# The order of attention's first loads, and where the second channel block's lag correlation is computed

## The chip, the cores and the metric

The kernel runs on one core of a Trainium2 chip. The metric is the device time of one launch in microseconds (us); the time given for a kernel is the median of its runs. The core has five engines that each work through their own list of instructions in order: TensorE (PE, matrix products), VectorE (DVE), ScalarE (ACT), GpSimd (POOL) and SyncE (SP, which does nothing but issue data transfers). A transfer (DMA) is issued by the queue of SP, ACT or POOL and then carried out by 16 DMA engines that all queues share. An instruction waits on semaphores for what it needs; what stands behind it in its list waits too.

## What is computed

The reference is a gated mix of two layers over the same input x (2048 positions, 576 channels), and the kernel returns the output and the gradient of every input for a given `grad_out`:

```python
def _A_ref(x, wqkv, wo):                       # attention, H = 32 heads of Dh = 18
    qkv = (x @ wqkv).reshape(B, S, 3, H, Dh).transpose(2, 0, 3, 1, 4)
    q, k, v = qkv[0], qkv[1], qkv[2]
    p = softmax(einsum("bhqd,bhkd->bhqk", q, k) * (Dh ** -0.5))
    o = einsum("bhqk,bhkd->bhqd", p, v)
    return o.transpose(0, 2, 1, 3).reshape(B, S, D) @ wo

def _B_ref(u, A_re, A_im, B_re, B_im, C_re, C_im, log_dt, Dskip):   # a state space layer, N = 128 states
    dt = exp(log_dt)[:, None]
    A = A_re + 1j * A_im;  Bc = B_re + 1j * B_im;  Cc = C_re + 1j * C_im
    P = exp((dt * A)[:, :, None] * arange(L))
    K = einsum("dn,dnl,dn->dl", Cc, P, dt * Bc).real     # one causal kernel of 2048 taps for each channel
    return causal_convolution(u, K) + u * Dskip

g = sigmoid((x * gate_w).sum(-1, keepdims=True))
out = g * _A_ref(x, ...) + (1 - g) * _B_ref(B_u, ...)
# returned: out, and the gradients of x, wqkv, wo, A_re ... Dskip and gate_w for grad_out
```

(The convolution is written with FFTs in the reference.)

## The kernel before

The kernel is one program of five stages. The order of instructions on each engine is written out by hand: in most of the kernel each engine runs what the source issues to it, in the order of the source.

**Stage s1** computes gate, queries, keys and values by matmuls on the transposed input, 24 steps in a row. The results are evicted by ACT and DVE to tiles `stg` and `qn` and stored in a DRAM tensor `QKV_d` (L409, L428) from the queues of ACT and POOL. Beside these steps run small jobs: the parameters of the state space layer (tiles `prm`, `zt`, `tp`, `Wn`, stored in `par_d` from POOL's queue), and `scale_go` (L293), which multiplies each 128-row tile of `grad_out` by g, for the gradient of attention, and by 1 - g. The second product, tile `xb`, is stored in DRAM in reversed order as `gyr_d` at L300: 16 stores of 144 KB from SP's queue. `gyr_d` is read later by the transfers that build `gyb_d` (in attention, from POOL's queue) and `RXn` (L592).

**Attention** goes through 32 units: 8 groups of 4 heads by 4 blocks of 512 queries. A unit has NST = 32 steps; NTOT = 1024 is the number of steps of all units. At each step G the forward pass computes one pair of score tiles (`ps_P<-QaT_g,KaT_g` on PE, Exp on ACT at L1382, then `accO` with the values `Vtok`). A second pass follows OFF = 39 steps later: transposed scores and Exp (L1387), the products with the output's gradient, `ds` on DVE (L1392), and the sums accV, accQ and accK. Part of each `ds` is transposed by a DMA on SP's queue (L1400, tile `dsT`), and accK waits for it. In the last unit the forward pass has ended: steps NTOT to NTOT + 62 hold only the second pass and the sums behind it. The operands of a group are loaded from `QKV_d` on SP's queue: `KaT` (keys with states on partitions, 4 tiles, `load_full`, L990 to L998), `QaT`, and `Vtok` (by a transposing DMA, `load_piece`). `at(("pre", G), f)` puts f at the head of step G; what has a time before step 0 is issued at once, in the order of its time. So the first loads on SP are KaT 0 to 3, Vtok 0, QaT 0, Vtok 1, Vtok 2.

**The S4 stage** treats the state space layer in 18 blocks of 32 channels. For each block b there is first its lag chain, which correlates x with the gated gradient at small lags, and which the rest of the block needs:

- `m_load(b)` loads `xs` (two transfers of 512 KB) and `gyp` (128 KB), L614 and L615;
- `m_part(b)` multiplies them on PE: 32 pairs of small matmuls into a PSUM tile `psM`; ACT copies it to `mst` (L628) and L629 stores that in DRAM (`Md_d`, 288 KB);
- `m_skw(b)` reads it back askew, in four transfers, as `skw` (L641);
- `m_sum(b)` sums it on PE with a 0/1 matrix, `misc<-sel,skw`;
- `m_fin(b)` puts the sums into two columns of `RX` on ACT (L652 to L654).

After that come `uv(b, 0)` and `uv(b, 1)` (PE `uvp<-RX,E1e`, ACT L708), which multiply the block's `RX` by the transposed basis `E1e` (made on PE by `turn_e` from `E1n`, which `load_en` or, for the first four halves, `en_first` loads in 4 pieces each); `scan_open(b)` copies the first column to `HG` (ACT, L714), and the scan on DVE (L733, L736, L738) runs over 15 segments. A block's second half of a scan runs together with the next block's first half. `xs`, `mst` and `skw` have one buffer each, `gyp` two.

Block 0's chain runs in attention's last unit: `m_load(0)` at NTOT + 15, `m_part(0)` at NTOT + 21 and `m_skw(0)` at NTOT + 25, and there the E1n pieces too (from NTOT + 23, one a step). `m_load(1)` comes at NTOT + 40, after the last of the `dsT` transposes. The rest of block 1's chain, and block 2's `m_load`, `m_part` and `m_skw`, are in the stage's prologue (L1452 to L1483), between the uv steps of blocks 0 and 1. From there on the loop over blocks keeps `m_part` and `m_skw` three blocks ahead of the scan and `m_load` four.

Of the kernel before, what the change touches and what calls it, by code (L numbers as in the profile page):

```python
# [20 lines left out]
def build(tc, aps, dbg_aps=None, stages=("s1", "attn", "post", "s4", "final")):  # L21
    nc = tc.nc
# [20 lines left out]
    NT = S // P  # L43
# [18 lines left out]
    with ExitStack() as gctx:  # L62
# [47 lines left out]
        gyr_d = dram.tile([P, NB, D], BF, name="gyr_d")  # L110
# [18 lines left out]
        with ExitStack() as ctx:  # L129
# [163 lines left out]
            def scale_go(b, q0):  # L293
                if q0 == 0:
                    dab[b] = s1.tile([P, TB, D], BF, tag="xr", bufs=4, name="d_a")
                for q in range(q0, q0 + 2):
                    t = b * TB + q
                    V.tensor_scalar(dab[b][:, q, :], xb[b][:, q, :], g_t[:, t:t + 1], None, op0=A.mult)
                    V.tensor_scalar(xb[b][:, q, :], xb[b][:, q, :], omg_t[:, t:t + 1], None, op0=A.mult)
                    nc.sync.dma_start(gyr_d[:, NT - 1 - t, :], xb[b][:, q, :])  # L300

            def da_turn(b, k, eng):
                if k < 2:
# [304 lines left out]
        def m_load(b, dma=nc.gpsimd.dma_start):  # L608
            xs = xss[b] = Q["pl"].tile([P, NSUB, SUB, CB], BF, tag="xs", bufs=1, name="xs")
            n = NSUB // 2  # L610
            for y in range(2):
                src = bass.AP(tensor=xb_d.tensor, offset=xb_d[b:b + 1, y * n:y * n + 1, 0:1].offset,
                              ap=[[XR * SUB * CB, NB], [SUB * CB, NSUB], [1, n * SUB * CB]])
                dma(xs[:, y * n:(y + 1) * n].rearrange("p e t c -> p (e t c)"), src)  # L614
            dma(Q["gyp2"][b % 2][:, SUB:2 * SUB, :].rearrange("p t c -> p (t c)"), gyb_d[b])  # L615
# [334 lines left out]
        if "attn" in stages:  # L950
# [5 lines left out]
            with ExitStack() as ctx:  # L956
# [33 lines left out]
                def load_full(g):  # L990
                    def piece(m):
                        t_ = grp_t.setdefault(g, {})["KaT", m] = ga.tile([P, KB], BF, tag="KaT", bufs=7, name="KaT_g")
                        nc.sync.dma_start(t_, strip("K", g, m * KB, KB))
                    for m in range(4):
                        if g == 0:
                            piece(m)
                        else:
                            at(("pre", 4 * NST * g + (16 if m == 3 else 6 * m - 59)), lambda m=m: piece(m))  # L998

# [121 lines left out]
                def at(n, f):  # L1121
                    todo.setdefault(n, []).append(f)
# [80 lines left out]
                def do_half(x):  # L1203
# [10 lines left out]
                    if odd:  # L1214
# [5 lines left out]
                        for y in range(2):  # L1220
                            nc.vector.tensor_copy(dOt[y][:, f0:f0 + fsz], dps[y][:, 0:fsz])
                            if u == 1:
                                nc.sync.dma_start(dO_d[:, t - 1 + y, :], dOt[y])

                load_full(0)
                lds = []
                for g in range(NG):
                    for m in range(4):
                        g0 = 4 * g * NST
                        lds += [(g0 + NST * m - 14, "QaT", g, m), (g0 + 8 * m - 18, "Vtok", g, m), (g0 + OFF + 8 * m - 18, "VaT", g, m),  # L1230
                                (g0 + OFF + 8 * m - 13, "Ktok", g, m), (g0 + OFF + NST * m - 14, "Qtok", g, m)]
                for g0, nm, g, m in sorted(lds):
                    if g0 < 0:
                        load_piece(nm, g, m)
                    else:
                        at(("pre", g0), lambda nm=nm, g=g, m=m: load_piece(nm, g, m))
# [33 lines left out]
                def en_first(b, h):  # L1270
                    enp[b, h] = load_en(b, h, nc.sync.dma_start, pieces=4)

                for x, f in ((15, lambda: pt_close("a", open_loads)), (15, lambda: m_load(0, nc.sync.dma_start)), (17, lambda: load_rx(0, nc.sync.dma_start)),
                             (21, lambda: m_part(0)), (23, lambda: pt_close("b", lambda: open_en(0))),
                             (25, lambda: m_skw(0)), (31, lambda: pt_close("c", lambda: open_en(1))),
                             (29, lambda: load_par(0, nc.sync.dma_start)), (33, lambda: load_par(1, nc.sync.dma_start)),
                             (OFF + NST // 16 - 1, lambda: m_load(1, nc.sync.dma_start))):
                    at(("pre", NTOT + x), f)
                for q, (b, h) in enumerate(((0, 0), (0, 1), (1, 0), (1, 1))):
                    at(("pre", NTOT + 23 + 4 * q), lambda b=b, h=h: en_first(b, h))  # L1280
                    for y in range(1, 4):
                        at(("pre", NTOT + 23 + 4 * q + y), lambda b=b, h=h, y=y: enp[b, h](y))
                for G in range(NTOT + OFF + 24):
                    now[0] = G
                    for f in todo.pop(("pre", G), []):
# [127 lines left out]
        if "s4" in stages:  # L1413
# [8 lines left out]
            with ExitStack() as ctx:  # L1422
# [27 lines left out]
                with tc.manual_schedule(engines={mybir.EngineType.SP}):  # L1450
# [6 lines left out]
                    turn_e(0, 0, 0, 4, dve_copy)  # L1457
                    m_sum(0)
                    m_fin(0)
                    uv(0, 0)  # L1460
                    prep_rx(1, dve_copy)
                    load_rx(1, nc.sync.dma_start)
                    turn_e(0, 1, 0, 4, dve_copy)
                    m_part(1)
                    m_skw(1)
                    m_load(2, nc.sync.dma_start)
                    uv(0, 1)
                    turn_e(1, 0, 0, 4, dve_copy)
                    scan_open(0)
# [1 line left out]
                    turn_e(1, 1, 0, 4)  # L1471
                    m_sum(1)
                    m_fin(1)
                    load_en(2, 1, nc.sync.dma_start)
                    uv(1, 0)
                    m_part(2)
                    m_skw(2)
                    uv(1, 1)
                    scan_open(1)
                    m_load(3, nc.sync.dma_start)  # L1480
                    prep_rx(2)
                    wk_cast(1)
                    for i in range(NBLK):  # L1483
# [387 lines left out]
```

## Time and profile before

| what | us |
|---|---|
| median of 3 runs | 2687.24 |
| lowest and highest run | 2683.43, 2697.16 |
| the profiled execution | 2685.73 |
| its span, first to last instruction | 2683.9 |
| PE busy in it | 2404.7 (90%) |
| ACT busy | 2350.8 (88%) |
| DVE busy | 2293.8 (85%) |
| POOL busy | 1818.0 (68%) |

The mean granted TensorE clock is 0.968 of the full one. On the time axis of the profiled execution, s1 ends near 120 us, attention runs from 131 to 2098, and the loop over blocks follows.

Some of the profile's views by stretch, as us of work in each window, with the clock granted to TensorE and the mean busy share of the DMA engines:

| window, us | PE | DVE | ACT | PE clock | DMA share |
|---|---|---|---|---|---|
| 118 to 120 | 0.67 | 1.36 | 1.10 | 1.00 | 0.37 |
| 121 to 131 | 0.09 | 0.00 | 0.52 | 0.50 | 0.94 |
| 131 to 141 | 9.97 | 1.65 | 5.92 | 0.50 | 0.03 |
| 141 to 160 | 18.32 | 5.85 | 15.35 | 1.00 | 0.35 |
| 2030 to 2096 | 44.84 | 40.25 | 31.12 | 0.66 | 1.10 |
| 2125 to 2131 | 4.79 | 1.55 | 2.88 | 0.51 | 1.03 |
| 2170 to 2192 | 20.89 | 21.40 | 20.27 | 1.00 | 0.83 |

A line of a timeline below has the start and the length of a group of instructions in us, the engine, the source line, the operation, the tiles written and read, and the count; in brackets stands how long the engine was idle before it and what ended the wait. The engines SPq, ACTq and POOLq in it are the queues that issue transfers. "L30" is the helper through which all matmuls go, so they are told apart by tile. A DMA share sums the times of packets, so it can go above 1.

### The profile page before, as it was taken

To read this page: it belongs to the slowest core of one execution; us is meant where nothing else is said; L and a number is where in the kernel's file an instruction comes from. 1 tells how busy PE (TensorE), PEld (TensorE's weight loads), DVE (VectorE), ACT (ScalarE), POOL (GpSimd) and SP (SyncE) were. 2 spreads that over 40 slices of the span, in tenths; PEclk is the share of its full clock that TensorE was granted. 3 is DMA by queue.
4 is the path that set the end of the run, shared out by engine and by line. 5 is a ranking of instruction groups with operands and counts; after the bars stand their busy time and mean duration, and the time that the engine had idled before them with its cause. 6 is when DMAs were issued, how large, how long until landed. Compare 5 with 4: busy or idle time off the path is not lost.

```text
span 2683.9 us, 69949 instructions
## 1 busy us (share of the span) xinstructions
PE 2404.7 (90%) x27411; PEld 1137.9 (42%) x27411; DVE 2293.8 (85%) x4090; ACT 2350.8 (88%) x2744; POOL 1818.0 (68%) x2829
## 2 busy tenths in 40 slices
PE   8799998998899899889888989989887699999999
PEld 4433333333333333333333333333232499998756
DVE  5648999999989999989999989989897589999964
ACT  5489999999999999999999999999995399999221
POOL 0278888888888888888888888887831045555431
PEclk9879999999999999999999999999996699999999
DMA  7637789879979978997898899789679889998895
GB/s 232 196 99 156 154 159 181 167 153 181 172 152 170 183 160 159 178 172 153 165 178 154 161 172 170 153 163 177 143 140 183 191 244 256 259 262 253 261 261 128
DMA packets 1157013, 486.63 MB, mean 181 GB/s; under 512 B 1071061, under 2 KB 1110598, under 8 KB 1154378
## 3 DMA queue, kind: packets, MB, share of 16 engines
q1 hardware_dynamic: 1110650, 341.49, 64.4%
q0 software_dynamic: 44016, 135.16, 18.3%
q10 hardware_dynamic: 2016, 5.51, 0.6%
q8 instruction: 214, 3.51, 0.6%
q14 instruction: 117, 0.96, 0.1%
HBM read 146.27 MB, written 93.80 MB: 89 GB/s over the span
## 4 chain that ended last, share of the span: by engine, by line
ACT 40%; PE 28%; DVE 18%; issue 6%; DMA 4%; POOL 2%; SPq 1%; ACTq 0%; DVEq 0%; POOLq 0%
ACT eb L1387 23%; ACT PT L1382 14%; DVE ds L1392 7%; PE ps_P L30 7%; PE accV L30 2%; PE ps_dx L30 2%; PE turn_p L1095 2%; PE ps_dwq L30 2%; DVE tz L733 2%; PE ps_proj L30 2%; DVE wab L753 2%; PE yp L30 2%; PE accK L30 1%; DVE dvacc L1149 1%; DVE tz L736 1%
## 5 line engine op out<-in xcount | busy, mean ns | idle before, releaser
L1392 DVE TENSOR_TENSOR ds<-ps_P,PT 128x512 bf16<-128x512 f32 x2048 | 1312.3, 683 | 125.5 <-PE ps_P L30 86.8
L1387 ACT ACTIVATE eb<-ps_P 128x1024 bf16<-128x1024 f32 x1024 | 1099.9, 1074 | 34.8 <-PE ps_P L30 34.5
L1382 ACT ACTIVATE PT<-ps_P 128x1024 bf16<-128x1024 f32 x1024 | 1105.0, 1080 | 21.7 <-PE ps_P L30 20.3
L30 PE MATMUL ps_P<-dOaT,VaT_g 32*128 32x512 bf16 x2048 | 581.9, 388 | 31.5 <-DVE ds L1392 16.1
L506 POOL TENSOR_TENSOR et<-eG,eT 128x448 f32<-128x448 f32 x576 | 542.2, 961 | 10.7
L30 PE MATMUL ps_P<-QaT_g,KaT_g 32*128 32x512 bf16 x2048 | 402.9, 386 | 136.5 <-ACT PT L1382 121.8
L30 PE MATMUL ps_P<-KaT_g,QaT_g 32*128 32x512 bf16 x2048 | 406.0, 389 | 1.6 <-ACT eb L1387 0.6
L30 PEld LDWEIGHTS <-KaT_g 32*128 32x128 bf16 x2048 | 147.6, 91 | 467.5 <-issue 451.4
L506 POOL TENSOR_TENSOR Eo<-et,et 128x448 bf16<-128x448 f32 x288 | 327.0, 1135 | 20.8
L30 PEld LDWEIGHTS <-QaT_g 32*128 32x128 bf16 x2048 | 116.1, 91 | 285.3 <-issue 262.4
L30 PE MATMUL accV<-eb,dOa 128*32 128x512 bf16 x2048 | 185.0, 394 | 27.2 <-ACT eb L1387 27.1
L30 PE MATMUL accO<-PT,Vtok_g 128*32 128x512 bf16 x2048 | 207.4, 394 | 0.0
L30 PE MATMUL accK<-dsT,Qtok_g 128*32 128x256 bf16 x4096 | 162.3, 279 | 14.5 <-DMA dsT<-ds 12.4
L30 PE MATMUL accQ<-ds,Ktok_g 128*32 128x512 bf16 x2048 | 161.6, 394 | 2.3 <-DVE dvacc L1149 2.2
L30 PEld LDWEIGHTS <-Vtok_g 128*32 128x32 bf16 x2048 | 52.7, 93 | 222.7 <-issue 222.7
L1100 DVE COPY dsT<-turn_p 128x1024 bf16<-128x1024 bf16 (+1 forms) x216 | 139.2, 644 | 2.1 <-PE turn_p L1095 2.1
L1095 PE MATMUL turn_p<-ident_bf,ds 128*128 128x128 bf16 x1664 | 134.1, 223 | 1.5 <-DVE gb L1167 0.8
L672 ACT COPY E1e<-etp 128x1024 bf16<-128x1024 bf16 x132 | 125.2, 1059 | 2.6 <-PE etp L671 2.6
L506 POOL TENSOR_TENSOR et<-eT 128x32 f32<-128x32 f32 (+3 forms) x288 | 115.9, 422 | 11.4
L1047 POOL TENSOR_TENSOR dOa<-dO_b,rl 128x288 bf16<-128x288 bf16 x32 | 21.5, 673 | 149.9 <-DVE rl L1042 149.9
L30 PEld LDWEIGHTS <-Qtok_g 128*32 128x32 bf16 x4096 | 87.9, 97 | 79.0 <-issue 64.0
L1095 PEld LDWEIGHTS <-ds 128*128 128x128 bf16 x1664 | 97.3, 99 | 49.5 <-issue 49.5
(294 smaller groups left out, 3749.3 us busy)
## 6 DMA issues: line engine op xcount, KB each, us to landing
E_d<-Eo POOLq DMA_DIRECT2D x144, 256.0 KB, 3.4
E1n<-E_d POOLq DMA_DIRECT2D x30, 1024.0 KB, 7.3
T0w<-Kp_d SPq DMA_DIRECT2D x18, 1024.0 KB
xs<-xb_d POOLq DMA_DIRECT2D x28, 512.0 KB, 9.8
dsT<-ds SPq DMA_TRANSPOSE x512
dqkv_d<-dtk POOLq DMA_DIRECT2D x96, 72.0 KB, 4.2
Md_d<-mst SPq DMA_DIRECT2D x18, 288.0 KB
skw<-Md_d SPq DMA_DIRECT2D x72, 64.0 KB
```

What stands on the lines that cost most here:

```text
L30: return nc.tensor.matmul(out, lhsT=lhsT, rhs=rhs, start=start, stop=stop, **kw)
L506: nc.gpsimd.tensor_tensor(out, a, b, op=op)
L672: copy(E_[:, 4 * q:4 * q + 4], pt_)
L733: nc.vector.tensor_tensor(tz[x], HG[:, :, k - 1].unsqueeze(1).to_broadcast([P, 2, 2, n, CB]), ZZ.unsqueeze(3).to_broadcast([P, 2, 2, n, CB ...
L736: nc.vector.tensor_tensor(tz[x][:, 0], tz[x][:, 0], UVk[:, :, :, k, :], op=A.add)
L753: nc.vector.tensor_tensor(wab, h_, w_, op=A.mult)
L1095: nc.tensor.transpose(pt_[:, x, qb, :], t_[:, qb * P:(qb + 1) * P], ident_bf)
L1100: (nc.scalar.copy if NTOT <= now[0] < NTOT + OFF else nc.vector.tensor_copy)(o_(), pt_[:, x:x + n])
L1149: nc.vector.tensor_tensor(o_, a_, acc, op=A.add)
L1382: nc.scalar.activation(U["PT"][i, j // 2], ps, ACT.Exp)
L1387: nc.scalar.activation(e, ps, ACT.Exp)
L1392: nc.vector.tensor_tensor(U["ds"][i][:, j, :], ps, U["PT"][i, j // 2][:, j % 2, :], op=A.mult)
```

## The change

There are three edits, and no instruction is added or taken away; all of them only move.

1. The 16 stores of `gyr_d` (L300) are issued from POOL's queue in place of SP's. In POOL's list 8 of them stand ahead of, and 8 behind, the three stores `par_d<-zt` and the `QKV_d<-stg` store beside them; all are ahead of the last `stg` store and of `par_d<-tp`.
2. The first loads of attention, on SP's queue, come as QaT 0, KaT 0, Vtok 0, KaT 1, KaT 2, KaT 3, Vtok 1, Vtok 2.
3. Block 1's lag chain is brought forward. In the last unit `m_load(1)` moves from NTOT + 40 to NTOT + 23, `m_part(1)` to NTOT + 31 (its `psM` takes the PSUM tile of `accO`, which is free there), and `m_load(2)` to NTOT + 33; the E1n pieces start one step later, the fourth half two. In the prologue `m_skw(1)` follows `m_fin(0)`, `m_part(2)` and `m_load(3)` stand where `m_part(1)`, `m_skw(1)` and `m_load(2)` stood, `m_skw(2)` follows `m_fin(1)`, and between `uv(1, 0)`, `uv(1, 1)` and `scan_open(1)` nothing is left.

```diff
@@ scale_go
-                    nc.sync.dma_start(gyr_d[:, NT - 1 - t, :], xb[b][:, q, :])
+                    nc.gpsimd.dma_start(gyr_d[:, NT - 1 - t, :], xb[b][:, q, :])
@@ load_full
                     for m in range(4):
                         if g == 0:
                             piece(m)
+                            if m == 0:
+                                load_piece("Vtok", 0, 0)
@@ attention, ahead of the steps
+                load_piece("QaT", 0, 0)
                 load_full(0)
...
                 for g0, nm, g, m in sorted(lds):
+                    if (nm, g, m) in (("QaT", 0, 0), ("Vtok", 0, 0)):
+                        continue
                     if g0 < 0:
                         load_piece(nm, g, m)
...
-                             (OFF + NST // 16 - 1, lambda: m_load(1, nc.sync.dma_start))):
+                             (23, lambda: m_load(1, nc.sync.dma_start)),
+                             (31, lambda: m_part(1)), (33, lambda: m_load(2, nc.sync.dma_start))):
                     at(("pre", NTOT + x), f)
                 for q, (b, h) in enumerate(((0, 0), (0, 1), (1, 0), (1, 1))):
-                    at(("pre", NTOT + 23 + 4 * q), lambda b=b, h=h: en_first(b, h))
+                    at(("pre", NTOT + 24 + 4 * q + q // 3), lambda b=b, h=h: en_first(b, h))
                     for y in range(1, 4):
-                        at(("pre", NTOT + 23 + 4 * q + y), lambda b=b, h=h, y=y: enp[b, h](y))
+                        at(("pre", NTOT + 24 + 4 * q + q // 3 + y), lambda b=b, h=h, y=y: enp[b, h](y))
@@ the S4 stage's prologue
                     m_fin(0)
+                    m_skw(1)
                     uv(0, 0)
...
-                    m_part(1)
-                    m_skw(1)
-                    m_load(2, nc.sync.dma_start)
+                    m_part(2)
+                    m_load(3, nc.sync.dma_start)
                     uv(0, 1)
...
                     m_fin(1)
+                    m_skw(2)
                     load_en(2, 1, nc.sync.dma_start)
                     uv(1, 0)
-                    m_part(2)
-                    m_skw(2)
                     uv(1, 1)
                     scan_open(1)
-                    m_load(3, nc.sync.dma_start)
```

## The prediction, made before the changed kernel was run

> **What bounds the kernel now.** I read the page first: span 2683.9 us, ACT 88%, PE 90%, DVE 85% busy, and a chain that ended last which is ACT's for 40% of it. These are averages; the change touches two short stretches, so I read each by itself: the timelines of SP, PE and ACT where the projections hand over to attention, then those of PE, DVE and SP where attention hands over to the blocks, then the table of windows for the granted clock.
>
> The first stretch on SP, then PE, then ACT (start, length, instruction, count, idle before it and who ended that):
>
> ```profile
> 71.82 32.34 SPq L300 DMA_DIRECT2D gyr_d<-xb  x16
> 106.92 13.07 SPq L993 DMA_DIRECT2D KaT_g<-QKV_d  x4
> 120.04 5.70 SPq L1008 DMA_TRANSPOSE Vtok_g<-QKV_d  x1
> 125.79 0.57 SPq L1004 DMA_DIRECT2D QaT_g<-QKV_d  x1
> ```
> ```profile
> 118.06 0.61 PE L30 MATMUL ps<-sq,hsel 126*128 126x512 bf16 x2
> 130.91 0.61 PE L30 MATMUL ps_P<-QaT_g,KaT_g 32*128 32x512 bf16 x4 [12.24 <-DMA QaT_g<-QKV_d]
> ```
> ```profile
> 120.23 1.28 ACT L1382 ACT_TABLE_LOAD   x1 [0.42 <-ACT qn L407]
> 131.56 2.85 ACT L1382 ACTIVATE PT<-ps_P 128x1024 bf16<-128x1024 f32 x3 [10.04 <-PE ps_P L30]
> ```
>
> PE stands still for 12.24 us because QaT_g, issued last but two, arrives at 130.8. It is issued at 125.79 because SP goes through its queue in order: 32.34 us of gyr_d stores that wait for VectorE's products, four keys, one Vtok transpose, then the queries. ACT has its table at 121.51 and waits 10.04 us more.
>
> The second stretch, PE and then DVE (here the lag chain of block 1 is run in the open):
>
> ```profile
> 2077.50 1.04 PE L30 MATMUL accK<-dsT,Qtok_g 128*32 128x256 bf16 x16 [6.27 <-DMA dsT<-ds]
> ...
> 2096.24 1.04 PE L30 MATMUL accK<-dsT,Qtok_g 128*32 128x256 bf16 x16 [4.92 <-DMA dsT<-ds]
> ...
> 2112.30 2.09 PE L30 MATMUL psM<-xs,gyp 128*32 128x128 bf16 x32
> ...
> 2123.24 0.39 PE L30 MATMUL misc<-sel,skw 128*128 128x8 f32 x2 [3.34 <-DMA skw<-Md_d]
> ...
> 2126.57 3.57 PE L30 MATMUL uvp<-RX,E1e 128*128 128x64 bf16 x32 [0.58 <-ACT dDs_row L654]
> 2130.61 2.11 PE L30 MATMUL psM<-xs,gyp 128*32 128x128 bf16 x32 [0.47 <-DMA gyp<-gyb_d]
> 2132.66 1.96 PE L30 MATMUL uvp<-RX,E1e 128*128 128x64 bf16 x32
> 2138.06 0.59 PE L30 MATMUL misc<-sel,skw 128*128 128x8 f32 x2 [3.44 <-DMA skw<-Md_d]
> ...
> 2145.94 2.13 PE L30 MATMUL psM<-xs,gyp 128*32 128x128 bf16 x32 [5.20 <-DMA gyp<-gyb_d]
> ```
> ```profile
> 2135.75 0.42 DVE L733 TENSOR_TENSOR tz<-HG,par 128x256 f32<-128x256 f32 x1 [9.17 <-ACT HG L714]
> ...
> 2162.83 0.42 DVE L733 TENSOR_TENSOR tz<-HG,par 128x256 f32<-128x256 f32 x1 [3.81 <-ACT HG L714]
> ```
>
> DVE, which is 21.40 of 22 us busy in the settled blocks (window 2170 to 2192), stands for 9.17 and 3.81 us. Its releaser is HG, which comes from uv (uvp), which comes after m_sum and m_part in PE's order. The two accK waits are attention's own: the transposed dsT is late from SP's queue.
>
> **Part 1, the start: gyr_d on GpSimd's queue, queries first.** Removed: 16 issues from SP. Added: 16 issues on POOL at 0.57 to 0.75 us (its other stores there), about 10 us, against 15.16 us of idle ahead of its store at 104.27 and 12.23 ahead of that at 120.05. Behind the waits of these stores stand POOL's stores of stg, zt and tp; the tp stores gate the table load at 120.23, and POOL could issue them at 106.18 with 14 us to spare (they landed by 117.3). So POOL's cost is 0, and if its cover fails, each us late beyond 3 is a us on the table load.
> On SP, QaT and the first KaT can now go when their buffers are released, after VectorE's last reading of zt (100.5 + 1.4), so at about 102 to 103 instead of 125.8 and 106.9. What remains is their transfer. KaT 0, issued at 107, landed between 119.4 and 123.3: 12 to 16 us, behind the stg stores in the same DMA engines (DMA share 0.94 in the window 121 to 131). Issued 4 us earlier behind QaT I put it at 118 to 123.5. PE is free at 118.7 and ACT at 121.51, so the first Exp falls between 121.5 and 124; I take 123.1, a gain of 131.56 - 123.1 = **-8.5**. Vtok 0 (step 3) now goes after KaT 0, the other keys are needed at step 8 and later (some 10 us on), so I charge them nothing; if KaT 1 were late as well, it would be a wait at step 8 instead.
> Bounds: -4 (KaT 0 lands at 127, when KaT 1 did in before) and -12.8: the full 10.05, and 2.8 for the clock. The windows show 0.50 granted from 121 to 141, after PE stopped at 118.7; the first unit's matmuls at half speed cost about 2.8 us there (pairs at 0.61 instead of 0.39 us). The drop came 1.8 us after the last matmul, so I expect it still to come, and take nothing. The first Exps after it ran at 0.50 until 141, 10.0 us after PE resumed at 130.91. The Trainium skill, TensorE: Matmul & The Clock Gate, Part 1: The HAM clock gate, gives about 3.4 us of work until the full clock is back; by the page those 2.8 would be about 1.0, and the term stays as it is. The gain is carried on through attention: its steps wait on one another, not on a clock time, and ACT paces them.
> The Trainium skill, DMA: Bandwidth & Descriptors, section Issuing engines are not separate DMA queues, speaks against this part: DMAs of scalar, sync and gpsimd run on the same 16 engines and interleave, and a second issuer saves sequencer time only. By it the gyr_d move would bring only what the order of issue does. The row of SP's 32.34 us is such sequencer time, with waits in it; the row of KaT 0's 12 to 16 us is the shared part, as the page would have it. This case's rows hold both.
>
> **Part 2, attention's last unit.** Added ahead of attention's last matmul: m_load(1) (at step NTOT+23 instead of +40), 32 psM matmuls and a copy at +31, a 288 KB store of Md_d, m_load(2) at +33. Moved one step later: the E1n pieces. Costs, by the rows of before:
> - PE: one psM, 2.09 to 2.13 us; it stands beside a wait of 0.78 before accV at that step, so +1.3 net, 2.1 without the cover. ACT: one mst copy 0.58, hidden (ACT is 31 of 66 us busy from 2030 to 2096).
> - SP: two m_loads (1.96 + 0.59 as at 2092.83, or 2.4 at 2035.42), Md_d 0.52. The first falls before the dsT transpose at 2065.86, 3.99 long of which 2.7 is waiting for VectorE: hidden. The others stand in the stretch from 2073.01 to 2100 in which SP issues without a pause: +2.5 + 0.5, less one or two E1n pieces (0.55 each) that slide behind, so +2.0 for everything queued after: the dsT transposes that both accK waits hang on.
> - DMA engines: share 1.10 in 2030 to 2096, no room. A 1.15 MB m_load took about 4.9 us of the ring (7.2 us from issue to landing at 2123.35). One of them before the last dsT (issued 2090.95, landed 2096.2): 3.3 to 6.8 us later with the SP term, if the ring is not empty by then.
> I take **+5** for the end of attention; bounds 0 (the transfers lie in PE's two waits, 6.27 and 4.92, and these do not grow) and +25 (psM waits 5.2 for its load, as at 2145.94; the ring adds two loads, 9.8; PE at half clock doubles some 10 us of matmuls).
>
> **Part 3, the first blocks.** Md_d(1) is stored long before, so skw(1) issued after m_fin(0) (2107) is there when m_sum(1) comes: the waits 3.34 + 0.48 + 0.15 go. The psM before uv(1,1) goes with its wait (2.11 + 0.47), as psM(2) takes psM(1)'s place at 2112.30; its data, m_load(2), was issued some 40 us before. m_load(3) and skw(2) are issued 10 to 15 us earlier than at 2135.57 to 2139.39, so the next m_sum and psM find theirs. Walked through: PE ends the transposes at 2119.9, m_sum 1.82 (as at 2104.63), but ACT has E1e copies until 2122.3, then m_fin 0.54, uv(1,0) at 2122.85, uv(1,1) 1.9 later, HG and scan 3.09 after its start (2132.66 to 2135.75): 2127.8. So the scan starts 7.95 earlier. In the next turn PE loses 3.44 and 5.20 of waits as well, so HG is no longer last and DVE runs at its own pace: scan to scan 21.9 (2162.83 to 2184.74), 2127.8 + 21.9 = 2149.7 against 2162.83: -13.1. As the transfers are squeezed into less time (share 1.03 from 2125 to 2131) I take **-12**; bounds -7.95 (the second wait stays) and -13.9 (DVE's 23.28 us of that turn less its two waits of 2.1).
> **Sum**: -8.5 + 5 - 12 = -15.5 against the profiled execution's 2685.73: 2670.2. That execution lies 1.5 below the median of the runs, 2687.24, so on the median's scale 2671.7, given as 2671.5. Something under 13.4 us (0.5%) can't be told from no change.
>
> **Rivals.**
> - A, the start's loads stay late: KaT 0's 12 to 16 us are the shared engines, and QaT now joins it there. For it: KaT landed 12 us after issue; against: ten more us. Start -4: 2676.2.
> - B, the last unit gives the blocks' gain back: for it, share 1.10 and 4.92 us of waiting on dsT already; against, dsT's late ones wait partly on ds itself. Last unit +14: 2680.7.
> - C, nothing is given back: -10, 0, -13.1: 2664.1. For it, SP's 2.7 us of slack and PE's two waits.
> - D, slower: the dsT transposes behind two m_loads make accK late by the full +25 while start and blocks give their low bounds, -4 and -7.95: +13, 2700.3. It decides the sign once the last dsT lands more than 12 us after 2096.2 (the gains' low bounds). Against: one of the two loads finds slack on SP.
> - E, POOL's stores are late and gate the table load, so part 1 does nothing: 0 + 5 - 12, 2680.2.
>
> **Numbers.** Forecast 0.46, A 0.13, B 0.17, C 0.16, D 0.04, E 0.04. The range is 2661 to 2684: C with the clock's 2.8 at the low end, B and a little beyond at the high one; D is left out. Under 2673.8 lie most of the forecast, C and little of the rest: faster 0.56, same 0.39, slower 0.05.
>
> **What would show it.** Start: QaT and KaT at about 103 on SP, the first ps_P before 124, ACT's 10.04 us gone. Last unit: psM at step NTOT+31 without a wait for gyp, accK's last wait under 10 us. Blocks: no wait on skw before misc, DVE's 9.17 under 2 and 3.81 under 1. Wrong if QaT still arrives after 127, if accK's waits grow by over 12 us together, or if HG stays the releaser.

## The result, and the profile after

| | before | changed |
|---|---|---|
| median of 10 runs each, us | 2689.32 | 2678.07 |
| lowest and highest | 2683.43, 2697.16 | 2667.38, 2691.14 |
| the profiled execution | 2685.73 | 2675.54 |
| its span | 2683.9 | 2673.6 |

The ratio (of the means of the runs) is 0.9959, with a 95% interval of 0.9942 to 0.9975: about 11 us faster. Run again later (below), the same kernel gave 0.9932 (0.9915 to 0.9949), and the two weighted by their 10 and 6 runs make 0.995, some 14 us. The forecast was 15.5 us. Single runs of either kernel differ by up to 24 us, so one profile is one draw from a wide spread. What its stretches show has to be checked on other executions, and that is what most of the runs below were for.

The start, in the timelines of SP, PE and ACT of the changed kernel (start, length, instruction, idle before it and its releaser):

```profile
102.03 0.35 SPq L1006 DMA_DIRECT2D QaT_g<-QKV_d  x1
102.48 2.63 SPq L993 DMA_DIRECT2D KaT_g<-QKV_d  x1
105.21 5.87 SPq L1010 DMA_TRANSPOSE Vtok_g<-QKV_d  x1
111.14 14.29 SPq L993 DMA_DIRECT2D KaT_g<-QKV_d  x3
```
```profile
120.61 0.61 PE L30 MATMUL ps_P<-QaT_g,KaT_g 32*128 32x512 bf16 x4 [1.86 <-DMA KaT_g<-QKV_d]
```
```profile
121.88 1.28 ACT L1388 ACT_TABLE_LOAD   x1 [1.99 <-DMA par_d<-tp]
123.18 2.86 ACT L1388 ACTIVATE PT<-ps_P 128x1024 bf16<-128x1024 f32 x3
```

PE's 12.24 us for QaT_g are 1.86 us for KaT_g, and the first Exp starts at 123.18 in place of 131.56. What ends last now is neither queries nor keys: ACT's table load waits 1.99 us for `par_d<-tp`, a parameter store that POOL issued at 106.81 and that landed at 121.8.

The end of attention and the first blocks, in PE's and DVE's timelines:

```profile
2062.58 2.19 PE L30 MATMUL psM<-xs,gyp 128*32 128x128 bf16 x32
...
2080.14 1.04 PE L30 MATMUL accK<-dsT,Qtok_g 128*32 128x256 bf16 x16 [8.34 <-DMA dsT<-ds]
...
2096.32 1.05 PE L30 MATMUL accK<-dsT,Qtok_g 128*32 128x256 bf16 x16 [4.25 <-DMA dsT<-ds]
2102.67 1.04 PE L30 MATMUL accK<-dsT,Qtok_g 128*32 128x256 bf16 x16 [5.30 <-DMA dsT<-ds]
...
2123.57 1.01 PE L30 MATMUL misc<-sel,skw 128*128 128x8 f32 x8
2126.57 5.36 PE L30 MATMUL uvp<-RX,E1e 128*128 128x64 bf16 x64 [2.00 <-ACT dDs_row L654]
...
2133.46 2.14 PE L30 MATMUL psM<-xs,gyp 128*32 128x128 bf16 x32
```
```profile
2132.97 0.43 DVE L733 TENSOR_TENSOR tz<-HG,par 128x256 f32<-128x256 f32 x1 [2.56 <-ACT HG L714]
...
2155.39 0.42 DVE L733 TENSOR_TENSOR tz<-HG,par 128x256 f32<-128x256 f32 x1 [1.22 <-ACT HG L714]
```

The psM of block 1 lies inside attention, at 2062.58, with no wait. The waits for skw and gyp ahead of uv(1) are gone (a later one of 0.32 us, for skw of block 2, is left), both halves of uv(1) stand together, and DVE's waits of 9.17 and 3.81 us are 2.56 and 1.22. Against that, accK now waits three times, 8.34 + 4.25 + 5.30, where it waited 6.27 + 4.92.

To compare executions, the span is cut at marks that every trace has: the first Exp, the first `eb` Exp (the second pass begins), the ACT copy of block 0's psM to `mst`, the last `dkacc` sum on DVE (attention ends, right after the last accK), and the `wab` product that follows the second joint scan. Lengths in us:

| stretch | before | changed | lag chain alone (e2) | both again (e5) |
|---|---|---|---|---|
| span's start to first Exp | 131.56 | 123.18 | 135.21 | 128.66 |
| first Exp to first eb | 51.41 | 50.33 | 51.39 | 52.48 |
| first eb to block 0's mst | 1863.49 | 1872.01 | 1869.49 | 1866.21 |
| mst to last dkacc (last unit) | 50.87 | 58.24 | 58.15 | 57.81 |
| last dkacc to second wab (first blocks) | 75.53 | 61.66 | 61.55 | 63.09 |
| second wab to the end | 511.00 | 508.15 | 507.96 | 508.79 |

The last unit and the first blocks repeat to within some 1.5 us: +6.9 to +7.4, and -12.4 to -14.0. One profile of the kernel before is a thin base for that, but e1, e3 and e4 below leave the lag chain where it was and add three: 51.5, 52.0 and 52.1 us in the last unit, 76.5, 76.8 and 74.2 in the first blocks. Against the mean of the four the last unit pays 6.2 to 6.6, the blocks gain 12.7 to 14.2, and the two together 6.5 to 7.7. The start and the body of attention do not, and the profile's own sum shows it: 8.4 gained at the start, 8.5 lost before block 0's psM.

### The profile page after: what moved, and what is told of

Same layout as the page of the kernel before. It is cut to its first block, busy times and chain, and to the rows that moved or that the text cites. A ratio compares the mean times of both kernels' runs of the same rounds, so it can differ in the third digit from the quotient of the medians.

```text
span 2673.6 us, 69952 instructions
## 1 busy us (share of the span) xinstructions
PE 2405.5 (90%) x27411; PEld 1134.6 (42%) x27411; DVE 2294.7 (86%) x4090; ACT 2352.0 (88%) x2744; POOL 1830.1 (68%) x2845
## 4 chain that ended last, share of the span: by engine, by line
ACT 39%; PE 28%; DVE 22%; issue 6%; DMA 3%; POOL 2%; SPq 1%; ACTq 0%; DVEq 0%; POOLq 0%
ACT eb L1393 23%; ACT PT L1388 14%; PE ps_P L30 8%; DVE ds L1398 7%; DVE tz L733 3%; DVE wab L753 3%; PE accV L30 2%; PE ps_dx L30 2%; PE turn_p L1097 2%; DVE tz L736 2%; PE accK L30 2%; DVE HG L738 2%; PE yp L30 2%; DVE Rw L758 1%; DVE dvacc L1151 1%
## 5 line engine op out<-in xcount | busy, mean ns | idle before, releaser
L30 PE MATMUL ps_P<-QaT_g,KaT_g 32*128 32x512 bf16 x2048 | 404.7, 387 | 126.6 <-ACT PT L1388 122.2
L1075 POOL COPY dtk<-gT 128x288 bf16<-128x288 bf16 x96 | 40.9, 426 | 107.6 <-DMA dqkv_d<-dtk 47.2
```

The costliest lines, as they stand in the source:

```text
L30: return nc.tensor.matmul(out, lhsT=lhsT, rhs=rhs, start=start, stop=stop, **kw)
```

## The experiments

Each run was timed beside the kernel before, in four groups, not all on one chip (e1 to e4; e5 to e7; e8 to e10; e11 and e12), so runs of different groups are compared by their ratios. The ratio has its 95% interval.

### The two parts of the start, and the lag chain, each by itself

e1_start has the edits 1 and 2 alone, e2_lag edit 3 alone, e3_order edit 2 alone, e4_gyr edit 1 alone:

```diff
# e1_start = before, with
-                    nc.sync.dma_start(gyr_d[:, NT - 1 - t, :], xb[b][:, q, :])
+                    nc.gpsimd.dma_start(gyr_d[:, NT - 1 - t, :], xb[b][:, q, :])
...
+                load_piece("QaT", 0, 0)
                 load_full(0)          # and Vtok 0 behind KaT 0
...
# e3_order: only the second part; e4_gyr: only the first
# e2_lag = the changed kernel with both undone
```

Expected of e1_start: 

> The two edits at the start alone, without the lag chain's move. Theory 1 (the parts add up): the first Exp falls near 123.2 as in the changed kernel, 8.4 earlier than in the one before, attention carries that on, and the time is 8 to 10 us below the one before. Theory 2 (the start's gain is given back inside attention, by longer stretches of TensorE's half clock): the first Exp is as early, but the half-clock stretches between 140 and 2100 sum to more than before's, and the time is only 1 to 4 us below.

Expected of e2_lag: 

> The move of block 1's lag chain alone, with the start as before. Theory 1 (the parts add up): the last accK of attention comes 5 to 8 us later against the step of block 0's psM than before, the second joint scan 14 to 16 us earlier than that, net 6 to 8 us below the one before. Theory 2 (the start's gain is given back): the whole of the measured 11 us is here, 9 to 12 us below.

Expected of e3_order: 

> The new order of the first loads alone, gyr_d still on SP's queue. Theory 1 (the order is what counts): the queries are issued at about 107, when the last gyr_d store has gone, and arrive by 122; the first Exp falls between 122 and 126, time 5 to 9 us below the one before. Rival (the queue is what counts): keys and queries arrive 4 to 5 us later than in the changed kernel, first Exp at 127 or later, under 4 us gained.

Expected of e4_gyr: 

> gyr_d's stores on GpSimd's queue alone, the loads in the old order. Theory 1 (the order is what counts): the queries still stand behind four keys and a transpose, of which the last key waits for a DMA semaphore until about 120, so the first Exp stays at 129 or later and the time within 3 us of the one before. Rival (the queue is what counts): queries by 122, 5 to 9 us below.

| run | median, us (before: 2690.73) | ratio | last qn store to first Exp, us |
|---|---|---|---|
| e1_start | 2681.10 | 0.9965 (0.9945 to 0.9986) | 126.58 to 130.53: 4.0 |
| e2_lag | 2681.08 | 0.9965 (0.9949 to 0.9982) | 119.89 to 135.21: 15.3 |
| e3_order | 2682.15 | 0.9976 (0.9956 to 0.9997) | 123.53 to 129.07: 5.5 |
| e4_gyr | 2689.18 | 1.0003 (0.9986 to 1.0020) | 119.82 to 133.07: 13.3 |

The start alone (e1) and the lag chain alone (e2) gain 9.4 us each, so the start's gain does reach the end. Theory 2 of e1 falls by the times, if narrowly (1 to 4 us were expected, 9.4 measured, the interval 3.8 to 14.8), and its body of attention, from the first eb Exp to block 0's mst, was as long as before: 1863.8 us against 1863.5. In e2 the time can't choose: 9.4, with an interval of 4.8 to 13.7, holds the 6 to 8 of Theory 1 and the 9 to 12 of Theory 2; its trace has 6.7 in the two stretches, as Theory 1 has it.

But the first Exp of e1's profile was expected at 123.2 and is at 130.5. The projections ahead of it ended late, their last qn store issued at 126.58 against 119.84 before; 1.8 us of that was there 32 us after the launch, before any changed instruction, and most of the rest is a wait of 6.09 us on ACT for an old `stg` store. POOL had issued that store at 106.21; it took 18.3 us to land, where it took 7.7 to 12.3 in the other profiles. Whether gyr_d's stores ahead of it in POOL's queue, or the early loads, had a part in this is not shown: e4, with the same queue, had no such wait, two later profiles (e7, e10) had 1.4 and 2.2 us of it for another stg store. Counted from the last qn store the handover takes 4.0 us, against 11.7 before, 15.3 and 13.3 in the other two with the old order of loads. So the move is worth 8 to 11 us at the place where it acts. Its yield is uneven because what comes ahead of it is.

Counted from the launch the gain is smaller: the first Exp comes at 131.6, 133.1 and 135.2 in the three profiles with the old order (mean 133.3), and at 123.2 to 131.4 in the six with both edits of the start, the tp stores on POOL and no idle matmuls (mean 128.3). That is 5 us, and the changed kernel's own profile is the earliest of the six.

The order of loads (e3) is the larger part of it: with gyr_d still on SP the handover takes 5.5, and the 6.4 us gained lie in the 5 to 9 of its Theory 1. Its places were missed: the queries were issued at 112.2 and not at about 107, and the first Exp came at 129.07, after the 122 to 126 of the theory and where the rival had it; this execution's projections also ended 3.7 us later than before's. The queue alone (e4) gives nothing, as its Theory 1 had it, for QaT_g still stands behind four keys. Whether gyr_d's move adds to the new order can't be told from 0.9976 and 0.9965.

### What the last unit pays

```diff
# e6_load2 = the changed kernel, with
-                             (31, lambda: m_part(1)), (33, lambda: m_load(2, nc.sync.dma_start))):
+                             (31, lambda: m_part(1)), (39, lambda: m_load(2, nc.sync.dma_start))):
# e7_en1 and e9_en1b = e6_load2, with the pieces of E1n of q = 2 and 3 (block 1) at
-                    at(("pre", NTOT + 24 + 4 * q + q // 3), lambda b=b, h=h: en_first(b, h))
+                    at(("pre", NTOT + (24 + 4 * q if q < 2 else 39)), lambda b=b, h=h: en_first(b, h))
...   (the other three pieces of each half likewise)
```

Step NTOT + 38 issues the last dsT transpose, so all that stands at NTOT + 39 is queued behind it. e5_both is the whole change again, on the same chip as e6 and e7; e9_en1b is e7's kernel once more, with a later group.

Expected of e5_both: 

> The whole change once more, beside the next two on one chip. Theory 1 (the parts add up; what its first profile showed lost inside attention was more time at TensorE's half clock in that execution): 14 to 19 us below the one before by the medians, and from block 0's psM to the last accK 57 to 59 us, from there to the second joint scan's end 61 to 62. Rival (the start's gain is given back whenever both are there): 8 to 12 us below, as measured first.

Expected of e6_load2: 

> The whole change, but m_load(2) issued behind the last dsT transpose (step NTOT+39 in place of +33). Theory 1 (m_load(2) ahead of the last transposes is most of what the last unit pays): from block 0's psM to the last accK 53 to 55 us in place of 58.2, the prologue after it as long as before (61.6 to the end of the second joint scan), 3 to 5 us below the whole change. Rival (the early psM and m_load(1) cost it): 56.5 or more, under 2 us gained. Rival 2 (m_load(2) then comes too late for psM(2)): a wait for gyp of over 2 us in the prologue, and nothing gained.

Expected of e7_en1: 

> As the run before it, and the 8 E1n pieces of block 1 too are issued behind the last dsT transpose (all at step NTOT+39). Theory 1 (whatever is queued on SP ahead of the transposes is paid by accK): 8 issues of 0.55 us and 2 MB less ahead of them, the last accK another 3 to 6 us earlier, 47 to 51 us after block 0's psM; the prologue waits for E1n by under 2 us; 8 to 10 us below the whole change. Rival (the transposes' own ds come last): accK no more than 1 us earlier than in the run before, and the E1n pieces late in the prologue, so slower than that run.

Expected of e9_en1b: 

> The kernel with m_load(2) and block 1's E1n pieces behind the last dsT transpose once more, beside the next two on one chip. Theory (that move is worth 8 to 10 us over the whole change): 22 to 28 us below the one before. Rival (the 26 us of the first time were a good draw): under 20 us.

| run | median, us | before, us | ratio | last unit | first blocks |
|---|---|---|---|---|---|
| e5_both | 2669.57 | 2687.86 | 0.9932 (0.9915 to 0.9949) | 57.81 | 63.09 |
| e6_load2 | 2671.50 | 2687.86 | 0.9938 (0.9919 to 0.9958) | 53.85 | 64.13 |
| e7_en1 | 2661.93 | 2687.86 | 0.9897 (0.9878 to 0.9916) | 48.29 | 62.20 |
| e9_en1b | 2665.61 | 2685.60 | 0.9930 (0.9905 to 0.9955) | 48.51 | 61.70 |

SP's timeline shows why. First before, from the third dsT transpose from the end on, then the changed kernel, then e6:

```profile
2083.37 1.75 SPq L1400 DMA_TRANSPOSE dsT<-ds  x1
2085.16 1.05 SPq L689 DMA_DIRECT2D E1n<-E_d  x2
2086.32 1.85 SPq L1400 DMA_TRANSPOSE dsT<-ds  x1
2088.22 1.34 SPq L689 DMA_DIRECT2D E1n<-E_d  x2
2089.66 1.20 SPq L1069 DMA_TRANSPOSE gT<-dkacc  x1
2090.95 1.82 SPq L1400 DMA_TRANSPOSE dsT<-ds  x1
```
```profile
2083.61 1.23 SPq L614 DMA_DIRECT2D xs<-xb_d  x2
2084.88 0.59 SPq L615 DMA_DIRECT2D gyp<-gyb_d  x1
...
2088.01 4.24 SPq L1406 DMA_TRANSPOSE dsT<-ds  x1
...
2092.97 3.12 SPq L1406 DMA_TRANSPOSE dsT<-ds  x1
...
2098.58 2.00 SPq L1406 DMA_TRANSPOSE dsT<-ds  x1
```
```profile
2084.43 1.46 SPq L1406 DMA_TRANSPOSE dsT<-ds  x1
...
2086.61 2.08 SPq L1406 DMA_TRANSPOSE dsT<-ds  x1
...
2091.91 2.20 SPq L1406 DMA_TRANSPOSE dsT<-ds  x1
2094.16 1.23 SPq L614 DMA_DIRECT2D xs<-xb_d  x2
```

m_load(2)'s own three issues take 1.9 us on SP, but the transposes behind it are slow to issue too: 4.24, 3.12 and 2.00 us where they took 1.75, 1.85 and 1.82, 3.9 us more together. This is not a wait for VectorE's ds: the last of those ended at 2087.28, before the first of the three was reached. e5 repeats it (4.50, 3.23, 1.58). In e6, with m_load(2) behind them, they take 1.46, 2.08 and 2.20, and the last unit is 4.4 us shorter than in the changed kernel: Theory 1 holds for the stretch. But the first blocks of e6 take 64.1 in place of the 61.6 that were expected, so 1.9 us are left of it. In e7 only gT transposes are left among the last dsT. PE's timeline of e7:

```profile
2078.40 1.04 PE L30 MATMUL accK<-dsT,Qtok_g 128*32 128x256 bf16 x16 [5.55 <-DMA dsT<-ds]
...
2091.18 1.90 PE L30 MATMUL accK<-dsT,Qtok_g 128*32 128x256 bf16 x32 [0.85 <-DVE dsT L1102]
...
2125.43 0.39 PE L30 MATMUL misc<-sel,skw 128*128 128x8 f32 x2 [3.72 <-DMA skw<-Md_d]
```

The two late waits on dsT by DMA are gone: the last 32 matmuls wait only for DVE. The last unit takes 48.3 us, less than the 50.9 of before although it holds one psM more, and the blocks behind it are no slower, except for a new wait of 3.72 for skw of block 2 that cost nothing measurable in the stretch. In the two stretches together that is 9.4 and 9.7 us less than the changed kernel's profile. The four later kernels (e8, e10, e11, e12) hold the same move; there the last unit takes 49.8 to 51.1, the two stretches together 111.5 to 114.1 in place of 119.9, so the gain repeats at 6 to 8. By the times, e6 did not show its 3 to 5 us (2671.50 against 2669.57), e7 showed 7.6 of the 8 to 10, and e9 came out 19.99 below the one before, short of the 22 expected and at the rival's bound of 20; its ratio of 0.9930 is about that of e5, 0.9932. Over both groups the ratio of this kernel is 0.991, against 0.995 for the change: about 10 us, with intervals of 5 to 7 us either way on e7 and e9. By the times alone the gain rests on e7, beside e5 in one group; the traces repeat it. e5 itself fell 18.3 below the one before, as Theory 1 had it, with 63.1 in place of 61 to 62 in the first blocks.

### TensorE's half clock, and the parameter stores

Each trace records the granted clock. The body of attention (first eb to block 0's mst) has some stretches at 0.50, and they differ from one execution to the next: near 175 to 206, near 1135, near 1890, near 2010. The clock column (PEclk, the third value from the end of a line: window, its length, busy us and counts of PE, PEld, DVE, ACT and POOL, clock, DMA share, GB/s) for the same windows, first before, then changed:

```profile
1125.00:1145.00 20.00, 18.40 (x195) 6.20 (x192) 17.88 (x31) 20.00 (x23) 17.12 (x23) 1.00 1.09 192
1885.00:1912.00 27.00, 23.77 (x224) 8.06 (x223) 21.56 (x38) 23.52 (x26) 25.02 (x40) 0.81 0.56 129
2008.00:2046.00 38.00, 33.61 (x303) 10.87 (x302) 29.55 (x49) 23.17 (x24) 4.53 (x9) 0.60 0.72 140
```
```profile
1125.00:1145.00 20.00, 16.74 (x169) 5.80 (x163) 14.96 (x25) 17.12 (x20) 11.54 (x16) 0.83 1.08 171
1885.00:1912.00 27.00, 24.99 (x206) 7.44 (x205) 18.85 (x32) 21.58 (x23) 24.96 (x32) 0.62 0.60 128
2008.00:2046.00 38.00, 34.81 (x294) 11.35 (x290) 27.98 (x45) 22.64 (x24) 3.59 (x8) 0.51 0.71 136
```

Summed over that body, and beside its length:

| execution | half clock, us | length, us |
|---|---|---|
| e8_warm | 41.5 | 1860.84 |
| e9_en1b | 47.4 | 1861.56 |
| e6_load2 | 53.4 | 1865.04 |
| before | 60.4 | 1863.49 |
| e1_start | 64.1 | 1863.80 |
| e4_gyr, e5_both, e7_en1 | 68.3 each | 1866.35, 1866.21, 1865.61 |
| e3_order | 78.3 | 1868.17 |
| e2_lag | 84.3 | 1869.49 |
| changed | 92.0 | 1872.01 |
| e11_tp | 95.6 | 1872.89 |

A line through these twelve (all profiles but e10 and e12, whose kernels have extra matmuls in attention) has the slope 0.22 us for each us at half clock and a correlation of 0.97. So the 8.5 us that the changed kernel's profile loses inside attention go with 31.6 us more of half clock (times 0.22: 6.9). Executions with the old order of loads (60, 68, 84) and with the new one (41 to 96) lie in one cloud: it looks like scatter, and not like something the earlier start brings about. The correlation alone does not say which way it goes: if something else holds the steps up, TensorE has longer gaps, and the clock may fall for that reason. That the clock is the cause was put to a test with idle matmuls:

```diff
# e8_warm = e7_en1, ahead of attention's first step
+                fill(accB("warm"), 16)
...
# e10_fill = e8_warm, and in the 32 steps after the first unit
-                                fill(acc, NFILL[nm])
+                                fill(acc, NFILL[nm] + (3 if NST <= G < 2 * NST else 0))
# e11_tp = e7_en1, the last three parameter stores (par_d<-tp twice, par_d<-wz)
-                    GP.dma_start(par_d[:, 4:5, :], tp[:, 0:1, :])
+                    AC.dma_start(par_d[:, 4:5, :], tp[:, 0:1, :])
...   (the other two likewise)
# e12_all = e10_fill with e11's stores and 8 matmuls in place of 16
```

Expected of e8_warm: 

> The same, with 16 idle matmuls (result unused) on TensorE between the projections' last matmul and the first scores. Theory 1 (TensorE's stop there halves the clock for the first 10 to 24 us of attention, and this is paid): the half-clock stretch that begins within 10 us of the projections' end is gone or at most 3.4 us, from the first Exp to the ninth 10.0 to 10.8 us in place of 11.5 to 14.2, 1 to 4 us below the kernel without them. Rival (ACT sets the pace there whatever the clock): the stretch goes and the ninth Exp comes no sooner after the first. Rival 2: the idle matmuls end after the keys' arrival and put the first Exp off by 1 us or more.

Expected of e10_fill: 

> The same as with the 16 idle matmuls, and in the 32 steps after the first unit three more idle matmuls ahead of each accV, accQ and accK burst. Theory 1 (half clock inside attention is scatter that comes of TensorE's gaps, and costs about 0.21 us for each us of it): the stretch of 17 to 27 us that begins near 175 shrinks to under 7 us, the first eb Exp to block 0's psM takes what 0.21 per us of half clock gives (1851.6 + 0.21 x half-clock us), 2 to 5 us below the run without these. Rival (the extra matmuls cost what they save, TensorE sets the pace there): no gain, or 1 to 5 us slower.

Expected of e11_tp: 

> The kernel with m_load(2) and block 1's E1n pieces behind the last dsT transpose, and the three stores par_d<-tp, par_d<-wz issued from ACT's queue in place of POOL's. Theory 1 (with gyr_d's stores ahead of them in POOL's queue the tp stores land late and are what now ends the wait before the first Exp): ACT's table load no longer waits over 1 us for par_d<-tp after its last qn (it waited 2.75 and 7.16 in the two profiles of this kernel with those stores on POOL), the first Exp comes 2 to 4 us after the last qn store's issue, 1 to 4 us below that kernel. Rival (the DMA engines are full whoever issues): the same wait within 2 us, or the stg stores behind them on ACT's queue land later and ACT's evictions wait instead.

Expected of e12_all: 

> All that gained so far together: that move of the tp stores, 8 idle matmuls ahead of the first scores and the three extra ahead of each burst of the second unit. Theory 1: the half-clock stretch after 120 gone or at most 3.4 us, the first Exp within 4 us of the last qn store's issue, 24 to 32 us below the one before. Rival (8 matmuls of some 2 us do not bridge the wait): a stretch of 10 us or more stays and the time is that of the run before it.

| run | median, us | before, us | ratio |
|---|---|---|---|
| e9_en1b, beside e8 and e10 | 2665.61 | 2685.60 | 0.9930 (0.9905 to 0.9955) |
| e8_warm | 2668.21 | 2685.60 | 0.9929 (0.9904 to 0.9955) |
| e10_fill | 2661.52 | 2685.60 | 0.9906 (0.9882 to 0.9930) |
| e11_tp | 2672.37 | 2689.91 | 0.9935 (0.9913 to 0.9956) |
| e12_all | 2668.91 | 2689.91 | 0.9928 (0.9900 to 0.9955) |

The window from 119 to 141, of e9_en1b and then of e8_warm:

```profile
119.00:141.00 22.00, 12.79 (x64) 4.78 (x63) 3.58 (x8) 10.14 (x11) 6.32 (x23) 0.69 0.65 112
```
```profile
119.00:141.00 22.00, 19.23 (x130) 8.16 (x129) 5.56 (x12) 15.20 (x16) 11.63 (x38) 1.00 0.49 128
```

The half-clock stretch after the projections is gone, and from the first Exp to the ninth it takes 8.99 us in place of 11.7 in e9; e12, with 8 idle matmuls, has 8.99 too. So the clock sets the pace there and the first rival falls. The second holds: the idle matmuls themselves put the first Exp off by 1.5 us (ACT waits that long for PE), so the net in the stretch is 1.2 us, and the times can't show it (e8's median is 2.6 us above e9's). Nor does the remedy always work: in e10, with the same 16 matmuls, PE then waited 3.11 us for Vtok 0, the clock was at 0.50 from 132.2 on for 10.2 us all the same, and the ninth Exp came 16.1 us after the first.

Inside attention the test failed. In e10 the stretch near 180 was 13.7 us long, not under 7 as expected, and its body of attention took 1864.6, 1.4 more than its 54.6 us of half clock would give by the line; e12's took 1871.0 with 61.4, 6.3 more than the line. e10's median is the lowest of its group, 6.7 us under e8, but the two intervals overlap, so it is inconclusive. That the half clock costs time inside attention is therefore argued from the correlation and from the start's stretch, and not shown.

e11 was aimed at the wait that took QaT_g's place. Lines of ACT's timeline in e9_en1b, then in e11_tp:

```profile
130.12 1.28 ACT L1388 ACT_TABLE_LOAD   x1 [7.16 <-DMA par_d<-tp]
```
```profile
107.36 0.37 ACTq L364 DMA_DIRECT2D par_d<-tp  x1
107.76 2.53 ACTq L365 DMA_DIRECT2D par_d<-tp  x1
110.32 1.13 ACTq L366 DMA_DIRECT2D par_d<-wz  x1
111.54 1.01 ACT L426 CAST stg<-ps_proj 126x1024 bf16<-126x1024 f32 x1 [8.44 <-DMA KaT_g<-QKV_d]
...
128.41 1.28 ACT L1388 ACT_TABLE_LOAD   x1 [0.50 <-ACT qn L407]
```

The table load's wait goes from 7.16 to 0.50, so the tp store was what it waited for. But ACT, which has evictions to do, now does none for 8.44 us: it works through its list in order, stands before the first of these issues until VectorE has finished tp at 107.3, and then takes 4.1 us to issue the three. The projections end 5 us later (last qn store at 127.94, against 122.99 in e9). The first Exp follows the last qn store sooner, after 1.8 us, but comes at 129.7, and by the ratio (0.9935, against 0.9930 and 0.9897) nothing is gained. The rival's second half has the outcome, a wait on ACT's evictions, though not its reason, stg stores that land late. In e12 the same edit keeps ACT from its work for 9.70 us and PE's projections with it, and the first Exp is at 135.1. Two parts of e12's theory held (no half clock after the projections, the first Exp 1.9 us after the last qn store), and its rival falls; the 24 to 32 us were missed, with 19 by the ratio.

## Why the prediction was right, and where it was not

The time was inside the range (2661 to 2684, measured 2678.07), the direction was right, and 11 to 18 us lie around the 15.5 forecast. The likelier bin was "faster by over 0.5%"; the first ten runs came out at 0.41%, inside 0.5%, the next six at 0.68%.

- **Start, -8.5.** In the profile the first Exp moved by -8.38, to 123.18 where 123.1 was named. The mechanism is right: over three profiles with the old order and nine with the new one (the tp stores on POOL in all) the handover after the last qn store took 11.7 to 15.3 and 3.3 to 8.4 us, and KaT 0 landed at 120.6, inside 118 to 123.5. That the number was hit to 0.1 us is luck: the average over profiles is 5 us, as the first Exp came later in the others. The step that failed is "POOL's cost is 0": the tp store landed at 121.8 (117.3 before) and gated the table load by 1.99 us here, and by 0.87 to 7.16 in the seven other profiles with both edits of the start and the tp stores on POOL. It was named as the price if the cover failed, and it is what ends last at the start now. From issue to landing this store took 13.9 to 20.5 us in the nine profiles with gyr_d on POOL, and 9.2, 10.6 and 15.6 with gyr_d on SP (e3, before, e2). So gyr_d's move goes with a later landing, but e2 waited 2.64 us for it without that move, so it is not the only cause. The rule of the Trainium skill that spoke against this part (DMA: Bandwidth & Descriptors, Issuing engines are not separate DMA queues) agrees with e4, where the queue alone brought a ratio of 1.0003.
- **The clock after the start.** The drop came as expected (at 120.5, for 10.2 us in place of 20.5), and was worth 0.5 us by the ninth Exp, which came 8.88 earlier. PE was back at work at 120.61 and the full clock at 130.8, 10 us later. The 3.4 us of sustained work of the Trainium skill (TensorE: Matmul & The Clock Gate, Part 1: The HAM clock gate) does not describe this stretch, in which PE works with gaps.
- **"The gain is carried on through attention"** holds by the times (e1: 9.4 us) and not by the one profile, whose body of attention was 8.5 us longer and had 31.6 us more of half clock. The scatter that this puts on every single execution, 12 us over twelve bodies of attention, was not in the prediction.
- **Last unit, +5.** Measured 7.4, 7.3 and 6.9. psM went in without a wait, as reckoned. What was under-sized is SP: m_load(2)'s own issues (2.5 us reckoned, 1.9 measured) and Md_d's (0.5 and 0.53) were right, but the transposes behind them lost 3.9 us in their issue, which was not a term of the sum; the prediction had only a later landing "if the ring is not empty by then". accK's waits grew by 6.7 us together, under the 12 that would have shown it wrong. Rival D's mechanism is this one, at a third of its price.
- **First blocks, -12.** Measured -13.9 and -14.0, and -12.4 in e5; the pace of DVE alone had given -13.1. But one of the prediction's own signs of being wrong is there: HG stays the releaser of both scans, after 2.56 and 1.22 us, where under 2 and under 1 were named. The step "HG is no longer last and DVE runs at its own pace" failed, by the 1.22 us. For the first scan ACT shows why: m_fin stands behind four E1e copies that end at 2126.1, and uv(1) waits 2.0 us for it after m_sum. For the second the cause of the 1.22 stays open. Most of the two waits, 9.2 of 13.0 us, did go with PE's new order.
- **Net of the two, -7**: -6.5, -6.7 and -5.5, or -6.5 to -7.7 against the mean of the four profiles with the old lag chain.

Of the rivals, B and C fall by the two stretches: the last unit pays 7 us, not 14 and not nothing. A falls by the handovers as a mechanism, but its price for the start, -4, is nearer to the average of 5 us than the forecast's -8.5. E falls by e1's time; its mechanism, a table load that waits for POOL's stores, is there at a part of its price.

## What to carry to other kernels

When a chain is brought forward into a busy stretch, look beyond its matmuls to the loads that it puts ahead of others in one queue, which were the larger part of its cost here. Look for the last transfer that somebody waits for, and queue everything else behind it (here that made the early chain nearly free: 48.3 to 51.1 us for the last unit in place of 58). When a late load is mended, list what else the same instruction waits for: the next in line, here a parameter store on another queue, decides how much of the gain is had. A gain of 0.3% can be lost from sight in a single profile when stretches of 10 us and more vary between executions, and it can also be hit there by luck; cut the span at marks and repeat the stretches.

## What was not expected of the hardware

- The half-clock stretches of TensorE come in steps of 3.4 us (3.4, 6.8, 10.2, 13.7, 17.1, 20.5, 23.9, 27.3 and so on up to 47.8 in these traces), begin while PE works with gaps (in the changed kernel near 175, in a stretch where PE waits 0.3 to 0.6 us at every other pair of scores) and not only after it stopped, and differ between executions of one program.
- The last three transposes by DMA held SP for 1.4 to 2.2 us each where no m_load was just ahead of them (before, e6, e7, e9), and for up to 4.2 and 4.5 us behind m_load's two 512 KB loads (the changed kernel, e5).
- The projections' end scatters too, from 119.8 to 126.6 by the last qn store (e11 and e12 aside). All profiles with the new order of loads but the first lie late (121.9 or more), those with the old one do not (119.8 to 119.9), although a part of the delay is there by 20 to 70 us, before any changed instruction has run. The clock records go with it: up to 100 us the four early executions have 6.8 us at half clock, the late ones 10.2 to 17.1, all but e8 with 6.8. Why the old order had none of the late ones is not explained.
